# Talking-heads attention and a squared-ReLU network on one core: more work in four 64x64 tiles of TensorE, and a new order of its units

## The chip, the cores and the metric

The kernel runs on one core of one Trainium2 chip, as one launch. The metric is the device time of one execution in microseconds (us); lower is better. The other cores are idle.

## The reference

Batch 8, 12 heads, 448 positions, head size 64; all inputs and the output are float32, and the kernel computes in bf16 with float32 sums.

```python
scores = scale * q @ k.transpose(0, 1, 3, 2)             # (8, 12, 448, 448)
scores = einsum('bhij,hg->bgij', scores, w_pre)          # mixes the 12 heads
attn   = exp(scores - max); attn = attn / (sum(attn) + 1e-9)
attn   = einsum('bhij,hg->bgij', attn, w_post)           # mixes the heads again
x      = (attn @ v) put together to (3584, 768)
h      = maximum(x @ w_in, 0.0)                          # w_in 768 x 2048
out    = (h * h) @ w_out                                 # w_out 2048 x 768
```

## The kernel before

**The stages of one batch.** The 448 query positions are cut into 45 chunks of 10 (CH); a chunk of 10 positions by 12 heads fills the partitions of one softmax block, and two chunks make a pair.

- T (emit_T, matmuls at L771 and L775): TensorE transposes q and k, 28 small transposes to a unit, six units a batch.
- QK (emit_QK, L924): scores of two heads at once for a tile of 128 queries, in two matmuls of 64 rows by 128 columns ("row": two tiles of the array, one above the other); the last 64 queries are done in four tiles of 64x64 ("quad"). ScalarE or VectorE evict them into `stage`.
- Relayout (emit_rel): a DMA issued from SP's queue takes each chunk from `stage` into `dring`, so that heads and positions share the partitions.
- Pre-mixing (emit_pre, L991): four matmuls of 64x64 ("quad") mix the heads of two chunks; ScalarE takes the exponentials with their sums (L1026).
- Post-mixing (emit_post, L1095): 14 short matmuls in two row tiles ("row") mix the heads after the softmax and transpose; the results go to `a2t`. VectorE takes the reciprocals, POOL or VectorE fold them into the weights (L1048, L1059).
- AV (emit_AV, L1157): attention times v. A unit makes two pairs of heads for 22 or 23 chunks (220 or 230 columns) in two tiles side by side of 128 rows by 64 columns ("cols"). The 448 keys are seven blocks of 64, held two and two on the 128 partitions in four slots; the odd block has half of its partitions filled with zeros, in `vraw` and in `vodd`, and is multiplied in two halves of the columns, so that a unit has 20 matmuls. One eviction of two copies follows (xt).
- F1 (emit_F1, L1230; L1209 for batches 0 and 1): x times w_in, ReLU (L1261 or L1262), square (L1271). From batch 2 on a unit has 12 matmuls in two row tiles ("row"); a pair of units sums two blocks of 128 outputs, in two phases in which the row tiles swap their two PSUM banks. For batches 0 and 1 it is "full": the whole array.
- F2 (emit_F2, L1351; L1299 for the last two tiles): h2t times w_out, four units of 16 matmuls ("row") to a tile of 128 tokens, in two phases as in F1; a DMA from POOL's queue writes the tile out.
- In batch 0 the first 22 chunks are made directly (emit_direct, L872, "full").

**What sets the order.** All of it is written out without loops on the chip. A planner (class _Plan) holds every piece as a task with its costs. TensorE's units stand in ten streams (0 transposes, 1 QK, 2 pre-mixing, 3 post-mixing, 4 AV, 5 direct, 6 and 7 F1, 8 and 9 F2), and the string ORDER names, digit by digit, from which stream TensorE takes its next unit. All other tasks are placed by the planner on ScalarE, VectorE, POOL or SP, in the order in which its estimates say that they come ready; tasks marked FLEX go to ScalarE or VectorE, whichever is to end first. The planner also gives each unit its PSUM banks, of eight (_Group, find), and holds estimates for the start and the rate of DMAs (DMA_START, DMA_AHEAD, dma_next), for a change of tiling (MODE_SWITCH) and for TensorE's instruction fetch (FETCH). These estimates are in no instruction: they only decide the order and the engine of the other tasks. Two phases of one sum that swap banks are held apart by a semaphore of TensorE on itself (`t.sync`).

## Time and profile before

| | us |
|---|---|
| median of 3 runs | 525.23 |
| the three runs | 523.72, 525.23, 532.38 |
| the profiled execution | 524.29 |
| its span, first to last instruction | 522.5 |
| TensorE matmul busy | 511.2 |
| ScalarE busy | 441.8 |
| VectorE busy | 423.5 |
| POOL busy | 210.6 |

The profiled execution has 1.79 us outside its span. "PE" is TensorE's matmuls, "PEld" its weight loads, "DVE" VectorE, "ACT" ScalarE, "POOL" GpSimd and "SP" the sync engine. Matmuls overlap in the array, and their ends are modelled, so that a row's duration is longer than what the matmul adds to the time: what a unit costs is read from the start of its first matmul to the start of the next unit. In a timeline row the columns are the start in us, the length in us from the first start to the last end, the engine, the line, the operation with its operands, and how many instructions are merged.

### The profile page before, as it was taken

Reading aid. Unit: us, or ns where it says so; the run is one execution under the profiler, and the core shown is the slowest. Engines: PE = TensorE matmul, PEld = TensorE weight load, DVE = VectorE, ACT = ScalarE, POOL = GpSimd, SP = SyncE. Lnnn points to the kernel's source line nnn. Section 1 sums busy time; section 2 is a strip of 40 time slices with the busy share of each in tenths; the row PEclk is TensorE's granted clock in tenths of the full one; section 3 lists DMA queues with packets and bytes.
Section 4 is the critical chain, followed back from the end, with each engine's and each line's share of the span. In section 5 each row is a group of like instructions: output and inputs, shape, how many; then the busy total and the mean of one; then the engine's idle time right before and its main releaser. Section 6 shows DMA issues by size and latency. Waiting matters only on the chain.

```text
span 522.5 us, 23105 instructions
## 1 busy us (share of the span) xinstructions
PE 511.2 (98%) x9467; PEld 323.7 (62%) x9467; DVE 423.5 (81%) x1181; ACT 441.8 (85%) x1265; POOL 210.6 (40%) x406
## 2 busy tenths in 40 slices
PE   8999999999999999999999999999999999999997
PEld 4455767567767565566456665557556575567874
DVE  7978989799999689978899779977899778967430
ACT  3689999989999898999999889989898898887411
POOL 9614445434642374135532366224643243133000
PEclk9999999999999999999999999999999999999999
DMA  8998999746985589556965599546974567442013
GB/s 157 198 213 160 199 191 195 163 101 134 173 175 115 121 162 178 117 131 140 188 116 109 139 169 182 123 89 148 178 137 102 130 154 132 92 102 63 3 26 101
DMA packets 82391, 71.90 MB, mean 138 GB/s; under 512 B 13371, under 2 KB 79659, under 8 KB 82283
## 3 DMA queue, kind: packets, MB, share of 16 engines
q0 software_dynamic: 36624, 32.81, 38.4%
q1 hardware_dynamic: 45370, 37.38, 29.8%
q8 instruction: 77, 1.26, 1.0%
q10 hardware_dynamic: 288, 0.20, 0.1%
q14 instruction: 32, 0.25, 0.1%
HBM read 45.70 MB, written 11.01 MB: 109 GB/s over the span
## 4 chain that ended last, share of the span: by engine, by line
PE 82%; ACT 10%; DVE 4%; DMA 2%; issue 1%; POOL 1%; SPq 0%; DVEq 0%; ACTq 0%
PE ps L1351 26%; PE ps L1230 20%; PE ps L991 6%; PE ps L1095 6%; PE ps L924 5%; PE ps L1157 5%; PE ps L872 5%; ACT pring L1026 4%; PE ps L1209 3%; ACT a2t L470 3%; PE ps L1299 2%; DMA dring<-stage 2%; PE ps L775 2%; ACT stage L470 1%; DVE stage L471 1%; ACT xt L470 1%
## 5 line engine op out<-in xcount | busy, mean ns | idle before, releaser
L1026 ACT ACTIVATE pring<-ps 128x448 bf16<-128x448 f32 (+1 forms) x368 | 195.4, 560 | 11.7 <-PE ps L872 5.8
L1048 POOL TENSOR_TENSOR wk2s<-wk2b,rinv 128x120 bf16<-128x120 bf16 x179 | 77.1, 433 | 196.4 <-DVE rinv L1041 195.4
L1351 PE MATMUL ps<-w_out_sb,h2t 64*128 64x384 bf16 x1664 | 152.1, 323 | 0.5 <-ACT pring L1026 0.3
L471 DVE CAST a2t<-ps 128x420 bf16<-128x420 f32 x180 | 113.4, 658 | 13.2 <-PE ps L1095 12.2
L1230 PE MATMUL ps<-xt,w_in_sb 64*128 64x448 bf16 (+2 forms) x1344 | 122.5, 323 | 0.2
L470 ACT ACTIVATE a2t<-ps 128x420 bf16<-128x420 f32 x180 | 109.2, 675 | 12.3 <-PE ps L1095 12.1
L471 DVE CAST stage<-ps 128x448 bf16<-128x448 f32 (+1 forms) x173 | 103.5, 616 | 10.2 <-PE ps L924 7.3
L1351 PEld LDWEIGHTS ps<-w_out_sb,h2t 64*128 64x128 bf16 x1664 | 78.8, 94 | 50.6 <-issue 2.8
L470 ACT ACTIVATE stage<-ps 128x448 bf16<-128x448 f32 (+1 forms) x187 | 96.4, 560 | 16.1 <-PE ps L924 15.5
L1230 PEld LDWEIGHTS ps<-xt,w_in_sb 64*128 64x128 bf16 x1344 | 61.2, 94 | 40.3 <-PE ps L924 1.2
L1026 ACT ACTIVATION_READ_ACCUMULATOR pring<-ps 128x1 f32 (+1 forms) x368 | 82.9, 225 | 0.0
L1384 POOL DMA_DIRECT2D out_dram<-osb x52 | 33.6, 652 | 98.3 <-DVE osb L471 32.6
L1095 PEld LDWEIGHTS ps<-wk2s,pring 60*128 60x128 bf16 x2160 | 51.8, 93 | 25.9 <-ACT pring L1026 3.2
L1095 PE MATMUL ps<-wk2s,pring 60*128 60x60 bf16 x2160 | 59.3, 187 | 1.9 <-POOL wk2s L1048 1.6
L1271 DVE TENSOR_TENSOR h2t<-h1t 128x448 bf16<-128x448 bf16 (+2 forms) x176 | 51.8, 323 | 5.2 <-ACT h1t L1261 4.7
L991 PE MATMUL ps<-dring,wk 64*64 64x448 bf16 (+1 forms) x676 | 53.5, 363 | 2.1 <-ACT pring L1026 1.0
L1059 DVE TENSOR_TENSOR ptail<-pring,rinv 128x128 bf16<-128x128 bf16 x169 | 50.7, 300 | 1.9
L1262 DVE TENSOR_SCALAR h1t<-ps 128x448 bf16<-128x448 f32 (+2 forms) x92 | 44.3, 481 | 9.8 <-PE ps L1230 7.1
L1261 ACT ACTIVATE h1t<-ps 128x448 bf16<-128x448 f32 (+2 forms) x84 | 38.3, 460 | 16.2 <-PE ps L1230 12.5
L1041 DVE RECIPROCAL rinv<-sums 128x2 f32<-128x2 f32 x184 | 28.8, 157 | 27.0 <-ACT pring L1026 25.7
L924 PE MATMUL ps<-qkt 64*128 64x448 bf16 (+1 forms) x360 | 50.1, 355 | 0.3 <-DVE qkt L471 0.2
L1209 PE MATMUL ps<-xt,w_in_sb 128*128 128x228 bf16 (+1 forms) x384 | 41.3, 260 | 0.4 <-ACT a2t L470 0.3
(72 smaller groups left out, 557.2 us busy)
## 6 DMA issues: line engine op xcount, KB each, us to landing
dring<-stage SPq DMA_DIRECT2D x309, 105.0 KB
out_dram<-osb POOLq DMA_DIRECT2D x52, 192.0 KB, 3.6
qraw<-in_q_dram POOLq DMA_DIRECT2D x42, 112.0 KB, 5.2
kraw<-in_k_dram POOLq DMA_DIRECT2D x42, 112.0 KB, 5.2
w_in_sb<-in_moe_w_in_dram POOLq DMA_DIRECT2D x8, 384.0 KB, 14.8
vraw<-in_v_dram POOLq DMA_DIRECT2D x24, 128.0 KB
w_out_sb<-in_moe_w_out_dram POOLq DMA_DIRECT2D x8, 384.0 KB, 9.5
vraw<-in_v_dram POOLq DMA_DIRECT2D x24, 96.0 KB
```

The costliest lines, as they stand in the source:

```text
L470: return eng.activation(o, i_, AF.Copy)
L471: return eng.tensor_copy(o, i_)
L924: r_ = eng.matmul(ps[y * w:(y + 1) * w, g.banks[x], 0:S], qkt[r0:r0 + 64, pb, p + y, 0, i0:i0 + w], qkt[r0:r0 + 64, pb, p + y, 1, :], star ...
L991: r_ = eng.matmul(ps[64 * y:64 * y + 64, gr.banks[x], 0:S], wk1[64 * x:64 * x + 64 - R0 * x, :], dring[64 * x:64 * x + 64 - R0 * x, (g0 + ...
L1026: return eng.activation(pring[0:r1, pr, 0:S], ps[0:r1, gr.banks[x], 0:S], AF.Exp, accum_out=sums[0:r1, g, :], **bias)
L1048: return eng.tensor_tensor(wk2s[:, p0:p0 + n, :], i0.to_broadcast([128, n, PR]), rinv[:, p0:p0 + n, :].to_broadcast([128, n, PR]), ALU.mult)
L1059: return eng.tensor_tensor(ptail[:, p0 // 2, :, :], pring[:, p0:p0 + n, 0:PJ], rinv[:, p0:p0 + n, :].to_broadcast([128, n, PJ]), ALU.mult)
L1095: r_ = eng.matmul(ps[:, gr.banks[x], o * PR:(o + 1) * PR], p_, w_, start=True, stop=True)
L1209: r_ = eng.matmul(ps[:, g.banks[0], 0:n], w_in_sb[:, ft, t * 128:(t + 1) * 128], xt[:, ft, c0:c1], start=(ft == 0), stop=(ft == NFT - 1))
L1230: r_ = eng.matmul(ps[:, g.banks[x], 0:n], w_in_sb[64 * y:64 * y + 64, ft, t * 128:(t + 1) * 128], xt[64 * y:64 * y + 64, ft, c0:c1], start ...
L1271: return eng.tensor_tensor(h2t[:, t16, o0:o0 + n], h1t[:, s, 0:n], h1t[:, s, 0:n], ALU.mult)
L1351: r_ = eng.matmul(ps[:, g.banks[hh], 0:FH], h2t[64 * y:64 * y + 64, t16, col:col + 128], w_out_sb[64 * y:64 * y + 64, t16, hh * FH:(hh + 1 ...
```

## The change

1. **Flexible tiling (`other`).** A QK unit of 128 queries, an F1 unit from batch 2 on and an F2 unit (but for the last two tiles) may run in "row" or in "quad". The planner decides when TensorE takes the unit: where the unit before was "quad", this one is "quad" too, with twice as many matmuls of 64 columns; else it stays "row".
2. **AV in quad.** A unit now makes one phase of two pairs of heads: the upper and the lower 64 partitions are separate row tiles that write to two PSUM banks, and a second unit swaps the banks behind a semaphore of TensorE on itself. The half-empty slot is no longer multiplied twice: 16 matmuls to a unit (four groups of four), three groups over all columns and one over half of them, two units where there was one. The unit holds two PSUM banks instead of one, and each pair of heads is evicted by a task of its own.
3. **Planner.** DMA_AHEAD from 3900 to 0, the rate of relayouts beside loads from 47.8 to 45.0, the estimates of the transposes and of w_out's loads; LATE is 0.0 and changes nothing.
4. **Batch 0.** The tiles of queries behind the direct part are 220 to 334 and 334 to 448 instead of 220 to 330 and 330 to 448, so that one chunk is moved by two relayouts.
5. **ORDER.** 998 digits instead of 950 (48 more AV units), all of them new.

```diff
-DMA_AHEAD = 3900.0
+DMA_AHEAD = 0.0
...
-    "0001155500055555555555555555115553115555313555500135555555533155335555511152533552020330"
...
+    "0001555010055555515555155515515553315315555135505551505115555555002353355553355555031213"
...
-                rate = (47.8 / (54.0 + b[2]), 0.72)
+                rate = (45.0 / (54.0 + b[2]), 0.72)
...
     def _commit_pe(self, t, start):
-        if t.mode != self.mode:
-            self.mode = t.mode
+        if t.other is not None and t.other[0] == self.mode:
+            t.mode, held, t.instrs = t.other
+            t.cost = {PE: (held, held + 190.0)}
+        self.mode = t.mode
...
-    NQ0 = 2
-    QT0 = tuple((CH * (ND + x * (NCH - ND) // NQ0),
-                 min(S, CH * (ND + (x + 1) * (NCH - ND) // NQ0))) for x in range(NQ0))
+    NQ0 = -(-(S - CH * ND) // IT)
+    QT0 = tuple((CH * ND + x * (S - CH * ND) // NQ0,
+                 CH * ND + (x + 1) * (S - CH * ND) // NQ0) for x in range(NQ0))
...
                     def fn_qk(eng, en, p=p, g=g, me=me, quad=quad):
                         r_ = None
+                        m = PJ if me[0].mode == "quad" else IT
                         for x, y in QUADS:
-                            if y * w < IT:
+                            if y * m < IT:
                                 r0 = 64 * x
+                                p_, i_ = (p + y, i0) if quad else (p, i0 + y * m)
                                 r_ = eng.matmul(
-                                    ps[y * w:(y + 1) * w, g.banks[x], 0:S],
+                                    ps[y * m:(y + 1) * m, g.banks[x], 0:S],
...
+                    if not quad:
+                        t_qk.other = ("quad", 205.0, t_qk.instrs + 4)
...
-                for p in range(0, NP, 2):
-                    g = _Group(1)
+                for p, ph in ((0, 0), (0, 1), (2, 0), (2, 1), (4, 0), (4, 1)):
+                    g = open_.setdefault(p, _Group(2))
...
+                        for s in range(NM + 1):
+                            for y, kk in QUADS:
+                                x = ph ^ y
+                                h = 2 * (p + x) + kk
+                                rows = slice(64 * y, 64 * y + 64)
+                                o_ = ps[kk * 64:kk * 64 + 64, g.banks[x], 0:w].rearrange(
+                                    "p (y n) -> p y n", y=2)
+                                a_ = a2t[half][rows, :, h, k0 * H5:k1 * H5]
+                                if s < NM:
+                                    a_ = a_[:, s::NM + 1, :]
+                                else:
+                                    a_, o_ = a_[:, NM, :], o_[:, y, :]
+                                v_ = vodd if s == NM and y else vraw[:, :, s, :]
+                                r_ = eng.matmul(o_, v_[rows, h, :], a_,
+                                                start=(ph == 0 and s == 0),
+                                                stop=(ph == 1 and s == NM))
...
-                                2 * NS * (w / 2.4 + 2.9) + 8.0, "cols", g, 4 * (NS + 1))
+                                3.5 * w / 2.4 + 25.0, "quad", g, 4 * (NM + 1))
+                    t_av.sync = before
...
+                        m = 64 if me[0].mode == "quad" else 128
                         for ft in range(NFT):
-                            for y in range(2):
+                            for y, z in QUADS:
+                                if z * m >= 128:
+                                    continue
                                 x = ph ^ y
-                                t = t16 + x
+                                t = (t16 + x) * 128 + z * m
                                 r_ = eng.matmul(
-                                    ps[:, g.banks[x], 0:n],
-                                    w_in_sb[64 * y:64 * y + 64, ft, t * 128:(t + 1) * 128],
+                                    ps[z * m:(z + 1) * m, g.banks[x], 0:n],
+                                    w_in_sb[64 * y:64 * y + 64, ft, t:t + m],
...
+                    t_h.other = ("quad", NFT * (n / 2.4 + 4.3) + 10.0, t_h.instrs + 4 * NFT)
...
+                        t_o.other = ("quad", nk * (FH / 2.4 + 3.7) + 10.0, t_o.instrs + 4 * nk)
```

F2's matmuls (fn_o) are cut in the same way as F1's.

More of the change, by code (lines that the diff above doesn't have):

```diff
@@ L19 @@
 SEM_LAT = 60.0
+LATE = 0.0
 MODE_SWITCH = 102.0
@@ L56 @@
                  "semval", "end", "order", "nwait", "succs", "clock", "avail", "mode", "dma",
-                 "done", "bias", "sync", "group", "instrs", "issued", "later", "two")
+                 "done", "bias", "sync", "group", "instrs", "issued", "later", "two", "other")
     def __init__(self, name, engine, fn, deps, after, cost, prio, sem, seminc, mode, dma,
@@ L81, in __init__ @@
         self.two = False
+        self.other = None
         self.bias = 0.0
@@ L121, in add @@
             mode=None, after=(), dma=None, group=None, instrs=0):
+        if engine not in (PE, SP):
+            cost = {e: (held, lat + LATE) for e, (held, lat) in cost.items()}
         t = _Task(name, engine, fn, deps, after, cost, prio, sem, seminc, mode, dma, group, instrs)
@@ L1470, in program @@
                 if b == 0:
-                    emit_load_w(1, [dir_done[c] for c in range(NDW)])
+                    emit_load_w(1, [dir_done[c] for c in range(min(ND, NDW))])
                     emit_load_v(b)
```

119 lines of the change are left out of this document (62 added, 57 removed).

## Prediction

> **What bounds the kernel now.** I read the page's busy times and chain first, then TensorE's waits, then the stretches, then timelines of TensorE.
>
> ```profile
> span 522.5 us, 23105 instructions
> ...
> PE 511.2 (98%) x9467; PEld 323.7 (62%) x9467; DVE 423.5 (81%) x1181; ACT 441.8 (85%) x1265; POOL 210.6 (40%) x406
> ...
> PE 82%; ACT 10%; DVE 4%; DMA 2%; issue 1%; POOL 1%; SPq 0%; DVEq 0%; ACTq 0%
> ```
>
> TensorE is busy for 98% of the span and 82% of the chain that ended last, so TensorE sets the end. Its named waits are few; the two longest kinds are these (total, times, longest):
>
> ```profile
> PE ps L1095 <- POOL wk2s L1048: 1.6, 2, 1.1
> ...
> PE ps L991 <- ACT pring L1026: 1.0, 1, 1.0
> ```
>
> By stretches (us, then busy of PE, PEld, DVE, ACT, POOL, the granted clock, the share of the DMA engines, GB/s):
>
> ```profile
> 60.00:120.00 60.00, 58.13 (x1113) 40.06 (x1107) 52.56 (x155) 56.38 (x168) 26.54 (x52) 1.00 0.83 164
> ...
> 240.00:300.00 60.00, 58.45 (x1181) 35.13 (x1179) 52.25 (x138) 56.00 (x159) 24.95 (x48) 1.00 0.69 137
> ...
> 480.00:522.00 42.00, 38.85 (x575) 29.77 (x569) 13.63 (x52) 12.07 (x31) 2.47 (x4) 1.00 0.18 47
> ```
>
> ScalarE is at 56 of 60 us in the middle, a close second there; VectorE has 7 to 8 us of 60 free. In the last 42 us TensorE is alone. The clock is full throughout.
>
> **The price of a change of tiling.** Start to start, in TensorE's timeline:
>
> ```profile
> 252.61 0.37 PE L924 MATMUL ps<-qkt 64*128 64x448 bf16 x2
> 252.80 1.32 PE L1230 MATMUL ps<-xt,w_in_sb 64*128 64x448 bf16 x12
> 253.94 0.37 PE L924 MATMUL ps<-qkt 64*128 64x448 bf16 x2
> 254.24 0.38 PE L991 MATMUL ps<-dring,wk 64*64 64x448 bf16 x4
> 254.56 1.31 PE L1230 MATMUL ps<-xt,w_in_sb 64*128 64x448 bf16 x12
> ...
> 258.84 0.57 PE L991 MATMUL ps<-dring,wk 64*64 64x448 bf16 x8
> 259.25 0.39 PE L775 MATMUL ps<-ident,qraw 64*64 64x64 bf16 x28
> 259.46 0.43 PE L775 MATMUL ps<-ident,kraw 64*64 64x64 bf16 x28
> 259.83 1.31 PE L1230 MATMUL ps<-xt,w_in_sb 64*128 64x448 bf16 x12
> ```
>
> A QK unit before another row unit takes 0.19 (252.61 to 252.80); before a quad unit it takes 0.30 (253.94 to 254.24), so the change costs 0.11. Two pre-mixings take 0.41 (258.84 to 259.25): 0.19 streamed, as the row pair of the same 448 columns, and about 0.02 more for the first group behind a change, whose weights were not loaded ahead. The way back, 254.24 to 254.56, is 0.32 less 0.21, again 0.11.
>
> How many changes: I walked ORDER, giving each digit its unit's tiling and, after, the rule of `other`. Before there are 255 changes, 94 of them into quad; after there are 195, 66 of them into quad (the label's 201 would hold the warm-up units, which are in no digit). So 60 fewer at 0.11 make **-6.6**, and 28 fewer first groups at 0.02 make **-0.6**. Bounds: the changes stand on the path only where TensorE would not have waited anyway, so 0 to -7.2.
>
> **AV.** Five units in a row of the batch at 424 us give the price:
>
> ```profile
> 424.17 0.52 PE L1157 MATMUL ps<-a2t,vraw 128*64 128x220 bf16 x8
> ...
> 424.95 0.50 PE L1157 MATMUL ps<-a2t,vraw 128*64 128x220 bf16 x8
> ...
> 426.51 0.52 PE L1157 MATMUL ps<-a2t,vraw 128*64 128x230 bf16 x8
> ...
> 427.31 0.52 PE L1157 MATMUL ps<-a2t,vraw 128*64 128x230 bf16 x8
> ```
>
> A unit takes 0.78 at 220 columns and 0.80 at 230, 0.79 on the mean. It streams eight widths (1800 columns at 225); the two new units stream seven (1575). A column costs 0.19/448 = 0.00042, so 1575 take 0.67; eight groups at 0.003 more give 0.69 to 0.70. 48 units by 0.09 make **-4.3**.
>
> But the second unit of a pair waits for the first's end. What this costs where nothing stands between shows in F1, where two units follow each other twice:
>
> ```profile
> 195.06 2.44 PE L1230 MATMUL ps<-xt,w_in_sb 64*128 64x448 bf16 x24
> 197.34 0.54 PE L924 MATMUL ps<-qkt 64*128 64x448 bf16 x4
> ...
> 208.88 2.62 PE L1230 MATMUL ps<-xt,w_in_sb 64*128 64x448 bf16 x24
> 211.34 0.25 PE L1095 MATMUL ps<-wk2s,pring 60*128 60x60 bf16 x6
> ```
>
> Two units of different sums take 2.28 (195.06 to 197.34); the two phases of one sum, held by the semaphore, 2.46: 0.18 more. In the new ORDER 6 of the 48 AV pairs follow directly; 28 have one unit of 0.19 between, which just covers it; the rest have more. 6 by 0.18 make **+1.1**; if the cover of 0.19 were short by 0.06, 28 more would add 1.7. Nothing but TensorE's own later units is queued behind that wait.
>
> **Quad for QK, F1 and F2.** By the same walk 51 more QK units, 43 F2 units, 34 F1 units of 448 columns and 12 narrow ones turn quad. QK and pre-mixing stream the same 0.19. For F1 and F2 the work is 43*8 + 46*6 = 620 groups of four where pairs stood. Their price in quad is nowhere in the trace; the rows that bear on it are the transposes above, the only long quad run: 28 with a weight load each, seven groups of four. The first unit takes 0.21 (259.25 to 259.46), 0.030 a group; both take 0.47 (to 259.83, less 0.11 for the change), 0.034 a group. 64 columns stream in 0.027, so a group costs 0.003 to 0.007 over its streaming; I take 0.006. The F2 pairs:
>
> ```profile
> 221.41 1.46 PE L1351 MATMUL ps<-w_out_sb,h2t 64*128 64x384 bf16 x16
> 222.71 0.73 PE L924 MATMUL ps<-qkt 64*128 64x448 bf16 x6
> ```
>
> Eight pairs in 1.30, 0.163 each for 384 columns (0.160 streamed): 0.003 over. The difference, 0.003 by 620, is **+1.9**. Ends: 0 if the pairs' price holds, and 620 by the 0.02 of an unprepared first group, +12.4. I take the transposes' value, since they are a run with loads in it.
>
> The page "TensorE: Matmul & The Clock Gate" of the Trainium skill (Part 3, packing small matmuls) says that a weight load runs beside a matmul in flight only in another row group; quad has two tiles in each. By that rule each group would pay its load, and the term would be the +12.4. The transposes at 0.030 to 0.034 do not bear it out; it stays as a rival.
>
> **Instruction fetch.** More matmuls mean more instructions for TensorE: 51*2 + 43*16 + 46*12 + 96*16 - 48*20 = 1918 matmuls, and as many loads, on 9467 of each: a fifth more.
>
> ```profile
> q8 instruction: 77, 1.26, 1.0%
> ```
>
> 77 packets for 18934 instructions are one for about 246; at some 518 us, 92.5 of them leave 5.6 us for each instead of 6.8. That TensorE can run out of code shows here:
>
> ```profile
> 201.47 0.19 PE L1095 MATMUL ps<-wk2s,pring 60*128 60x60 bf16 x1
> 201.83 0.38 PE L1095 MATMUL ps<-wk2s,pring 60*128 60x60 bf16 x11 [0.17 <-issue]
> ```
>
> A post-mixing stops inside its unit, where no semaphore is waited for, for 0.36 where 0.03 is usual. The fetch queue from 89.5 to 105.5 us, and from 195 to 205 us:
>
> ```profile
> q8 instruction: 4, 0.07, 1.7%
> ```
>
> ```profile
> q8 instruction: 2, 0.03, 1.4%
> ```
>
> Four packets in 16 us, one in 4, were in time; in the busier stretch around the stop two in 10 us, one in 5, were not. Walking ORDER with the durations above and cutting every 246 instructions, stretches shorter than 4.0 us add up to a lack of 2.4 us before and 8.4 after; of the 2.4 I find about 1 in the trace, since waits lengthen dense stretches. 1/2.4 of 8.4 is **+3.5**. Ends: 0, and a bound for AV alone: its 96 units of 32 instructions fill 12.5 packets at 0.35 a unit, 2.7 us each where 5 are needed: 2.3 by 12.5 = +29.
>
> The page "Runtime: NRT & Kernel Launch" of the Trainium skill (Instruction fetch mechanics) calls the crossing of such a block mostly hidden. By that the term is 0 and the sum 3.5 lower; the stop at 201.47 is one that was not hidden.
>
> **Waits.** Pre-mixings that follow one another wait for ScalarE's exponentials to free banks:
>
> ```profile
> 75.33 0.38 PE L991 MATMUL ps<-dring,wk 64*64 64x448 bf16 x4
> 76.76 0.38 PE L991 MATMUL ps<-dring,wk 64*64 64x448 bf16 x4 [1.04 <-ACT pring L1026]
> ```
>
> ORDER has 72 direct successions of pre-mixings before and 37 after, since flexible units now stand between. I take a little over half of the 2.6 us of waits quoted at the start: **-1.5**. Ends -4 and +5: AV holds two banks for one, and ScalarE has little room.
>
> **Costed at nothing.** AV's evictions are as many copies as before, of 220 or 230 columns each, shared by two engines and off the path:
>
> ```profile
> L471 DVE CAST xt<-ps x54: 370/395/415, 49.2 to 456.0; 128x220 bf16<-128x220 f32 x30, 128x230 bf16<-128x230 f32 x24
> L470 ACT ACTIVATE xt<-ps x42: 368/408/505, 50.7 to 486.5; 128x230 bf16<-128x230 f32 x24, 128x220 bf16<-128x220 f32 x18
> ```
>
> Were the cover gone, a unit would stand 0.4 us for its bank. One relayout more in batch 0 goes to SP's queue, which holds 309 of the largest kind:
>
> ```profile
> dring<-stage SPq DMA_DIRECT2D x309, 105.0 KB
> ```
>
> It stands beside the direct matmuls of batch 0; uncovered it would cost one pre-mixing's wait, under 1 us. POOL's loads keep their chain. The planner's other estimates move tasks between engines, not their number.
>
> **Sum.** -6.6 -0.6 -4.3 +1.1 +1.9 +3.5 -1.5 = -6.5 against the profiled execution's 524.29 (span 522.5 and 1.79 around it): 517.8. That execution is 0.94 under the median 525.23, so the forecast for a median is 518.7, 1.2% less.
>
> **Rivals.**
> - Fetch is hidden and the waits shrink by 4: 518.7 - 3.5 - 2.5 = 512.7. For it: before, almost all fetches are hidden, and fewer bursts of pre-mixing. Against it: a fifth more code.
> - ScalarE becomes the bound from 60 to 300 us, with 56 of 60 busy: what is saved in those 240 of 522 us (46% of 11.5, about 5) turns into waits: 523.7. Against it: VectorE's free 7 to 8 us, and FLEX.
> - Every quad group pays its weight load: 518.7 + 12.4 - 1.9 = 529.2. Against it: the transposes.
> - Slower: AV in quad outruns the fetch. Two AV units take 0.70 with 64 matmul and load instructions, where one took 0.79 with 40. At the full 29 instead of 3.5 it is 544; from 10 us of stops on it is slower than before, from 20.5 on by over 2%. Against it: 41 AV units stand alone and 20 runs have two, with longer units between.
>
> **How the numbers follow.** Forecast 0.43 (its own range 515 to 523), hidden fetch 0.32, ScalarE 0.12, weight loads 0.07, fetch stops 0.06. Faster by over 2% (under 514.7; 2% is about what a measurement of this kernel can tell from no change) is the second case, 0.32; slower by over 2% (over 535.7) is the last, 0.06; within 2% the other three, 0.62. The range 509 to 530 leaves out the last case and the lower part of the second.
>
> **What would show each step.** The page after should list about 11400 matmuls and 92 packets in the fetch queue. Right: quad F2 units of 32 matmuls at 1.30 to 1.34; AV units at 0.33 to 0.36; a timeline with fewer gaps of 0.11; chain and busy share of TensorE still near 98%. Wrong: F2 quad units at 1.45 (loads exposed), many idle times of TensorE ended by "issue" inside a unit (fetch), or waits of TensorE for ScalarE's evictions in the hundreds of nanoseconds from 60 to 300 us. The sum falls if TensorE's busy time sinks as said but its waits grow by as much.

## The result, and the profile after

The changed kernel takes 533.65 us in the median of four executions, three of them between 532.74 and 533.79; the kernel before takes 526.37 beside it: a ratio of 1.0136, interval 1.009 to 1.0182. One execution took 1263.08 us (as one of dry_nosync's twelve below took 1262.55), at a full clock and for a cause that is not known; the ratios leave these two out, and the median of the other three is 533.51. The change makes the kernel slower by 1.4%, and the time lies above the range that was given. The profiled execution took 532.74 us, 8.45 more than the profiled one of before (524.29), and 14.9 more than the sum of the prediction (517.8).

The page of the changed kernel, the lines that answer to those shown of before:

```profile
span 531.0 us, 26929 instructions
...
PE 508.6 (96%) x11380; PEld 334.0 (63%) x11380; DVE 429.8 (81%) x1184; ACT 443.4 (84%) x1267; POOL 207.9 (39%) x401
...
q8 instruction: 92, 1.51, 1.1%
...
PE 3%; ACT 0%; DVE 0%; issue 0%
```

The counts are as forecast (about 11400 and 92): 11380 matmuls, 92 packets of code. TensorE's busy time fell by 2.6 us although it has 1913 matmuls more, while the span grew by 8.5: TensorE has less to do and stands still longer. The chain breaks off a few per cent from the end in this trace (3% of TensorE and nothing else), so it carries nothing here; what stands still has to be read from TensorE's own rows.

TensorE's waits in the changed kernel (total, times, longest):

```profile
PE ps L1260 <- issue: 4.5, 5, 1.6
PE ps L1109 <- issue: 3.0, 2, 2.3
...
PE ps L1388 <- issue: 1.1, 2, 0.9
PE ps L1174 <- issue: 0.8, 1, 0.8
```

Before, the longest kinds, the warm-up's apart, were waits for POOL and for ScalarE. Now the first places belong to "issue", that is to stops in which no semaphore was waited for, and they fall on every kind of work: here F1, post-mixing, F2 and AV, each once or a few times, and in rows below these QK and transposes. A cause that strikes whatever stands there is hardly in any one of these units.

Stretches of the changed kernel (busy of PE, PEld, DVE, ACT, POOL, the clock, the share of the DMA engines, GB/s):

```profile
60.00:120.00 60.00, 59.08 (x1303) 41.52 (x1305) 54.00 (x161) 57.32 (x177) 25.93 (x52) 1.00 0.84 159
...
240.00:300.00 60.00, 56.50 (x1376) 36.54 (x1369) 52.05 (x135) 52.97 (x153) 24.89 (x50) 1.00 0.69 134
```

From 60 to 120 us TensorE is busier than before (59.1 against 58.1). From 240 to 300 us it loses 2.0 us of busy time against before, and ScalarE, which was to be the rival bound there, falls from 56.0 to 53.0. So ScalarE did not become the bound: it does less in the same time, as it would if TensorE held it up.

Now the place itself, TensorE's timeline of the changed kernel:

```profile
253.52 0.54 PE L1260 MATMUL ps<-xt,w_in_sb 64*128 64x448 bf16 x3
254.51 1.11 PE L1260 MATMUL ps<-xt,w_in_sb 64*128 64x448 bf16 x9 [0.45 <-issue]
...
257.48 1.31 PE L1260 MATMUL ps<-xt,w_in_sb 64*64 64x448 bf16 x24
258.62 0.36 PE L1005 MATMUL ps<-dring,wk 64*64 64x448 bf16 x4
...
260.56 0.19 PE L1109 MATMUL ps<-wk2s,pring 60*128 60x60 bf16 x2
261.43 0.23 PE L1109 MATMUL ps<-wk2s,pring 60*128 60x60 bf16 x4 [0.68 <-issue]
...
262.82 1.32 PE L1260 MATMUL ps<-xt,w_in_sb 64*128 64x448 bf16 x12
264.07 0.38 PE L1005 MATMUL ps<-dring,wk 64*64 64x448 bf16 x4
...
264.91 1.13 PE L1260 MATMUL ps<-xt,w_in_sb 64*64 64x448 bf16 x20
266.82 0.38 PE L1260 MATMUL ps<-xt,w_in_sb 64*64 64x448 bf16 x4 [0.78 <-issue]
...
272.77 0.28 PE L782 MATMUL ps<-ident,qraw 64*64 64x64 bf16 x11 [0.63 <-issue]
```

An F1 unit stops after 3 of its 12 matmuls, a post-mixing after 2 matmuls of a run of 6, an F1 unit after 20 of 24, a transpose after 17 of 28. Counted in the order in which TensorE gets its loads, matmuls and semaphore instructions, all 14 long stops without a semaphore (steps of over 0.3 us from one matmul to the next, the warm-up left out) stand at the same place modulo 256, to one instruction (at the 193rd or 194th of each 256). 256 instructions are what one packet of the fetch queue brings (16.4 KB of 1.51 MB in 92 packets). So these read as stops at the end of the code that is there; the packets, next, bear it out.

The same 6.9 us between two such borders, 254.51 and 261.43, in the DMA view of the changed kernel: first up to 259.1, and then the microsecond from 259.1 on.

```profile
q0 software_dynamic: 716, 0.43, 74.7%
q1 hardware_dynamic: 459, 0.38, 28.4%
```

```profile
q0 software_dynamic: 162, 0.09, 72.4%
...
q8 instruction: 1, 0.02, 5.5%
```

For 4.6 us after the border no code moves: the first view has no row of q8 at all, the DMA engines are full of the POOL queue's loads (q0, 75%) and the relayouts (q1, 28%). The packet comes at 259.13, lasts 0.88, and TensorE goes on 1.42 after its end. Such a fetch takes 6.9 us; at its start TensorE had 6.0 us of work left (254.51 to 260.56).

**The ledger.** For every group of matmuls I took the time from its start to the next one's and laid it down as streamed work (columns by 0.00042, and up to 0.03 a group above it), as a change of tiling (up to 0.125 where the tiling differs), as a stop (at a 256th instruction, no semaphore), as a wait (the next group has a semaphore to wait for), or as other. The span is 5.4 us longer than each sum in these two kernels: what lies ahead of the first matmul and behind the last. In us:

| | streamed | changes (number) | stops (number) | waits | other | sum |
|---|---|---|---|---|---|---|
| before | 474.5 | 27.8 (263) | 0.4 (2) | 12.5 | 1.9 | 517.1 |
| after | 472.8 | 20.8 (201) | 12.7 (14) | 17.8 | 1.4 | 525.5 |
| difference | -1.7 | -7.0 | +12.3 | +5.3 | -0.5 | +8.4 |

The change did what it says, for 8.7 us, and lost 17.6 to code that came late and to waits.

### The profile page after: what moved, and what is told of

The parts are those of the page before. It is cut to its first block, busy times and chain, and to the rows that moved or that the text cites. A ratio compares the mean times of both kernels' runs of the same rounds, so it can differ in the third digit from the quotient of the medians.

```text
span 531.0 us, 26929 instructions
## 1 busy us (share of the span) xinstructions
PE 508.6 (96%) x11380; PEld 334.0 (63%) x11380; DVE 429.8 (81%) x1184; ACT 443.4 (84%) x1267; POOL 207.9 (39%) x401
## 3 DMA queue, kind: packets, MB, share of 16 engines
q8 instruction: 92, 1.51, 1.1%
## 5 line engine op out<-in xcount | busy, mean ns | idle before, releaser
L1040 ACT ACTIVATE pring<-ps 128x448 bf16<-128x448 f32 (+1 forms) x368 | 197.6, 565 | 12.7 <-PE ps L1005 7.9
L1388 PE MATMUL ps<-w_out_sb,h2t 64*64 64x384 bf16 (+1 forms) x2352 | 153.8, 323 | 1.3 <-issue 1.1
L478 DVE CAST a2t<-ps 128x420 bf16<-128x420 f32 x196 | 122.8, 659 | 11.3 <-PE ps L1109 10.3
L1260 PE MATMUL ps<-xt,w_in_sb 64*64 64x448 bf16 (+5 forms) x1896 | 124.9, 324 | 4.6 <-issue 4.5
L1388 PEld LDWEIGHTS ps<-w_out_sb,h2t 64*64 64x64 bf16 (+1 forms) x2352 | 88.1, 101 | 41.6 <-issue 2.3
L477 ACT ACTIVATE a2t<-ps 128x420 bf16<-128x420 f32 x164 | 100.0, 675 | 11.0 <-PE ps L1109 10.1
L1260 PEld LDWEIGHTS ps<-xt,w_in_sb 64*64 64x64 bf16 (+1 forms) x1896 | 67.5, 101 | 38.6 <-issue 6.6
L1005 PE MATMUL ps<-dring,wk 60*64 60x448 bf16 (+1 forms) x676 | 59.8, 360 | 1.2 <-DVE stage L478 0.4
L1293 ACT ACTIVATE h1t<-ps 128x448 bf16<-128x448 f32 (+2 forms) x102 | 45.6, 469 | 18.2 <-PE ps L1260 16.4
L936 PE MATMUL ps<-qkt 64*64 64x448 bf16 (+1 forms) x460 | 54.4, 355 | 1.5 <-issue 0.7
L1174 PE MATMUL ps<-a2t,vraw 64*64 64x230 bf16 (+3 forms) x1344 | 46.8, 253 | 1.6 <-issue 0.8
L1294 DVE TENSOR_SCALAR h1t<-ps 128x448 bf16<-128x448 f32 (+2 forms) x74 | 36.6, 496 | 13.1 <-PE ps L1260 11.4
```

Of the source, the lines that this page charges most:

```text
L477: return eng.activation(o, i_, AF.Copy)
L478: return eng.tensor_copy(o, i_)
L936: r_ = eng.matmul(ps[y * m:(y + 1) * m, g.banks[x], 0:S], qkt[r0:r0 + 64, pb, p_, 0, i_:i_ + m], qkt[r0:r0 + 64, pb, p_, 1, :], start=True ...
L1005: r_ = eng.matmul(ps[64 * y:64 * y + 64, gr.banks[x], 0:S], wk1[64 * x:64 * x + 64 - R0 * x, :], dring[64 * x:64 * x + 64 - R0 * x, (g0 + ...
L1040: return eng.activation(pring[0:r1, pr, 0:S], ps[0:r1, gr.banks[x], 0:S], AF.Exp, accum_out=sums[0:r1, g, :], **bias)
L1174: r_ = eng.matmul(o_, v_[rows, h, :], a_, start=(ph == 0 and s == 0), stop=(ph == 1 and s == NM))
```

## The experiments

Two theories at first. **Code:** the stops are the loss; the new kernel runs the same work through a fifth more instructions, and the fetch does not keep up. **Waits:** TensorE's waits, above all AV's second phase behind its first and AV's two banks, set the pace; a stop only takes up time that would be waited out anyway. The first eight runs take out one part each; the other eight take the two suspected costs away. The kernel before ran beside each of the five groups of runs, on the same chip (medians 525.75, 525.65, 526.37, 526.61 and 525.16); the ratios are to it.

**1. Code alone.** The kernel before, with each F2 matmul cut into two of 192 columns: 1664 matmuls and as many loads more, no change of order, of tiling or of sums.

```diff
-                                for y in range(2):
+                                for z, y in ((0, 0), (0, 1), (1, 0), (1, 1)):
+                                    c = z * FH // 2
-                                        ps[:, g.banks[hh], 0:FH],
+                                        ps[:, g.banks[hh], c:c + FH // 2],
```

> The kernel before, with each matmul of F2 (L1351) cut into two of 192 columns: the same work in the same tiling and order, but 1664 more matmuls and as many weight loads, 3328 instructions more, nearly as many as the change adds (3826). Theory (TensorE runs out of code): the array itself pays about 832 groups at 0.0025 = 2 us; the fetch queue goes from 77 to 90 packets, and stops inside units at every 256th instruction appear, 6 to 12 us in all: 533 to 540. Rival (the new order or the quad tiling makes the loss, not the amount of code): 528 to 529, and no more stops than before.

Measured: 532.21 us, ratio 1.0101 (1.0031 to 1.0171); profiled span 531.7. The ledger against before: streamed +2.0, stops +8.0 (9 of them), waits -0.2. The waits of TensorE in this kernel:

```profile
PE ps L1352 <- issue: 2.8, 3, 1.4
PE ps L1230 <- issue: 2.3, 1, 2.3
PE ps L1095 <- POOL wk2s L1048: 1.6, 2, 1.1
```

The stops are in the range that was forecast (6 to 12), the time is just under its own (533 to 540). Two rows of "issue" have put themselves ahead of the wait for POOL that led before. Instructions alone, with 90 packets for 77, bring the stops. The longest (2.3 idle, at 324.25 us) is not in F2, whose matmuls were cut, but in an F1 unit as it was: it is the border that is paid for, whatever unit stands there.

**2. Less traffic beside the code.** From batch 2 on, the loads of q, k and v bring one row each; in the changed kernel and in the one before. The lines for v are shown; q and k are cut alike. The rest of that data is left out.

```diff
+                    if b >= 2:
+                        i_ = bass.AP(v.tensor, (b * H + h0) * S * D + t0 * D,
+                                     [[NT * D, 1], [S * D, 4], [1, D]])
+                        o = vraw[64 * u:64 * u + 1, h0:h0 + 4, 0, :]
```

> The changed kernel, whose loads of q, k and v from batch 2 on move a single row in place of the whole (the rest of q, k and v of these batches is left out; all instructions stay). Theory (the code's packets stand behind the loads of POOL's queue): the time from a block's border to its packet falls to about 1 us, the 13 us of stops at borders fall below 4, and the time falls to 519 to 524. Rival A (fetch has a time of its own that loads do not touch, the code is simply too much): stops stay at 10 us or more, 528 to 534. Rival B (the stops are only where waits would be anyway): stops vanish, but the time stays over 529.

> The kernel before with the same light loads (q, k and v of batches 2 to 7 left out but for one row). It had under 1 us of stops, so by the fetch theory it gains only what lighter transfers give to relayouts: 522 to 526, and the changed kernel with light loads is to lie 0 to 6 us below it, as the forecast without fetch had it. If it gains as much as the changed kernel does (10 us), the loads cost both kernels by another way than fetch.

Measured: after 530.16, ratio 1.0083 (1.0054 to 1.0113); before 524.82, ratio 0.9991 (0.9967 to 1.0015). The stops of the changed kernel fall from 12.7 to 5.9, its waits go from 17.8 to 18.7. So about half of the stops comes from the loads that move beside the code; the relayouts (q1) are left as they were. The theory's time (519 to 524) did not come, and its stops (below 4) not quite: the time lies where both rivals had it. A part of the 5.3 us between the two light kernels is the granted clock, the share of its full clock that TensorE was allowed: 0.990 to 0.997 in every execution of light_after, 0.999 or more in eight of ten of light_before.

**3. The row tiling alone.** The changed kernel and its order, with `other` left out, so that QK, F1 and F2 always run in rows; AV stays in quad.

```diff
-                        t_qk.other = ("quad", 205.0, t_qk.instrs + 4)
+                        t_qk.other = None if True else ("quad", 205.0, t_qk.instrs + 4)
```

(one of three such lines; the same in F1 and F2)

> The changed kernel with flexible tiling taken out (QK, F1 and F2 always in row tiles), AV in quad and the new ORDER kept: 370 changes of tiling instead of 195, and 2684 instructions fewer. Theory: stops at borders fall from 13 to about 3 us, the 175 changes at 0.11 bring back 19 us, which makes 540 to 545: the flexible tiling does save its changes, and pays for them in code. Rival (quad units are slow in themselves): under 534.

Measured: 541.04, ratio 1.0288 (1.0216 to 1.0359). Against after: changes +19.3 (376 for 201), stops -9.0, waits -1.6, streamed -1.6. The time is as forecast (540 to 545). In this order the flexible tiling saves 19.3 us of changes, and pays 10.6 for it in stops and streamed work.

**4. An order that leaves the code time.** The changed kernel; digits of ORDER were moved about by the planner's own reckoning with a longer fetch (4.7 us), until few borders were short. One of ORDER's twelve lines is shown; all were changed.

```diff
-    "2336372010716233627100726123673137424424002922391391119118333832282182192239139133931414"
+    "2336372100716233617200712623672137434420240922391119319118333832281282192239339131931412"
```

> The changed kernel with an ORDER of its own: digits were moved about while the planner's FETCH held a fetch at 4.7 us and more in place of 4.0, with the rest as it is. It has 222 planned changes of tiling instead of 201 and as much code. Theory (the planner took fetch as too short, and its order put dense code where the code was late): stops at borders fall from 12.7 to under 6 us, 21 changes more cost 2.3, so 527 to 530. Rival (the amount of code makes the stops, in whatever order): stops stay over 9 us, 533 or more.

Measured: 533.19, ratio 1.0167 (1.0118 to 1.0217). The stops are down to 1.7 (forecast: under 6), the waits up from 17.8 to 24.6, changes +2.5; the time is the rival's (533), not the theory's (527 to 530). TensorE's waits in this kernel:

```profile
PE ps L1005 <- ACT a2t L477: 1.1, 3, 0.5
PE ps L936 <- DVE h1t L1294: 0.9, 1, 0.9
...
PE ps L1260 <- issue: 0.8, 1, 0.8
```

Here the theory of the code alone fails: an order that gives the fetch time puts units beside each other that wait for banks and for the engines that empty them. Avoided by order, the stops turned into waits.

**5. The parts alone.** Three kernels, each with an order moved by the same search: the kernel before as it is (a control for the search), the kernel before with AV in quad, and the changed kernel with before's AV and quad only where no row unit comes next. Of each edit only the lines that tell it are shown.

```diff
 order_alone: before, ORDER moved
 avq_alone:   before + quad AV
+                for p, ph in ((0, 0), (0, 1), (2, 0), (2, 1), (4, 0), (4, 1)):
+                    g = open_.setdefault(p, _Group(2))
 flex_alone:  after - quad AV, and
+                elif then == "row":
+                    t.other = None
```

> The kernel before with nothing but its ORDER moved about in the same way, as the control for the other three: 291 planned changes instead of 263. 28 changes cost 3.1 if nothing else moves; theory: waits fall by about as much, 523 to 529.

> AV in quad without flexible tiling: QK, F1 and F2 as before, the ORDER of before with 48 digits for AV's second units, moved about in the same way. 292 planned changes, 1171 instructions more than before. Theory (the two phases of AV wait for each other and for their two banks, and save 3 us of streaming): 29 changes +3.2, streaming -3, waits +2 to +5, stops under 3: 528 to 534. Rival (AV gains the 4.3 us of the forecast, the loss is flexible tiling's): 521 to 526.

> Flexible tiling without the new AV: AV as before (cols, 20 matmuls to a unit), QK, F1 and F2 in quad only where the next unit of fixed tiling is not row; the ORDER of before, moved about in the same way. 276 planned changes (263 before), 412 instructions more than before. Theory: with so little more code the stops stay under 2 us; 13 changes cost 1.4: 524 to 529. Rival (quad is slow in itself or makes waits): over 531.

Measured: the control 528.77, ratio 1.007 (1.0041 to 1.0099); AV in quad 535.19, ratio 1.0181 (1.0145 to 1.0217); flexible tiling 532.55, ratio 1.0149 (1.0089 to 1.0209). The control is where it was forecast (523 to 529), the other two lie above their forecasts (528 to 534, 524 to 529). No order that I found by the planner's reckoning is as good as the one before had, so neither part can be called worth a gain or a loss by the ratio alone. The ledgers say more: the kernels split by their AV. Every kernel with AV in quad had waits of 16 to 25 us up to here (after 17.8, light_after 18.7, rows_only 16.2, order_fetch 24.6, avq_alone 21.4); every one without has 11 to 15 (12.5, 11.9, 12.3, 14.8, 10.9). As the orders differ as well, this is a pattern and not a proof.

**6. The wait between AV's phases.** In both phases each row tile takes the bank of its own number, so the second need not wait for the first; order, placement and instructions stay. The sums then lack the terms of the other row tile.

```diff
-                                x = ph ^ y
+                                x = y
-                    t_av.sync = before
+                    t_av.sync = []
```

> The changed kernel; in both phases of an AV unit each row tile takes the bank of its own number (x = y), so that no two row tiles ever add into one bank, and the second phase no longer waits for the first. The order, the planner's placement and every instruction's size are as in the changed kernel (the sums lack the terms of the other row tile, so half of each product is left out of its place). Theory (the wait for the first phase's end is a cost of its own on TensorE's path): the waits of AV behind AV (1.7 us, 11 of them) and of AV behind a pre-mixing that stands between the phases (0.7 us, 12) vanish, TensorE's waits fall from 17.8 to about 15.4, and the median from 533.6 to about 531.2. Rival (TensorE's waits are set by the engines that free its banks; the phase wait only takes up time that would be waited out a little later): the waits move to the next bank, and the median stays at 533 to 534.

> As the run before it, and in addition the q, k and v loads of batches 2 and above bring one row each instead of all (the rest of that data is left out), as in the earlier run with light loads at 530.2. If the stops for code and the phase waits are separate costs on one path, this kernel stands 2.4 below that: about 527.8, and still above the kernel before with light loads (524.8), by the remaining stops of 5.9 us. If both only hide other waits, it stays at 529.5 to 530.5.

> The changed kernel in the order moved so that TensorE rarely runs out of code (stops 1.7 us, waits 24.6, 533.2), with the same edit of AV: no wait between the phases. There AV behind AV waits 2.8 us (13 times) and AV behind a pre-mixing 0.5. Theory of separate costs: about 530 us. Rival, that the waits are those of the banks whatever the order: 532.5 to 533.5, with TensorE's waits still at 23 or more.

Measured: nosync 537.71, ratio 1.0185 (1.0123 to 1.0247), light 530.23, ratio 1.0079 (1.0051 to 1.0107), in the order of 4 534.11, ratio 1.0146 (1.0094 to 1.0197). By the medians none is faster than its counterpart with the wait (533.65, 530.16, 533.19). AV's own waits did go: AV behind AV from 1.73 to 0.79 us in nosync, from 2.82 to 0.16 in fetch_nosync. But TensorE's waits in all stayed within 0.5 us of what they were in both, so other units waited instead, as the rival had it; and the stops grew: 12.7 to 16.2, 5.9 to 8.5, and 1.7 to 5.3. TensorE's timeline of nosync, at the F1 unit that stopped at 254.51 in the changed kernel:

```profile
256.43 0.54 PE L1260 MATMUL ps<-xt,w_in_sb 64*128 64x448 bf16 x3
258.59 1.11 PE L1260 MATMUL ps<-xt,w_in_sb 64*128 64x448 bf16 x9 [1.62 <-issue]
```

It is the same matmul; the step to it from the matmul before is 1.97 us for 0.80. A likely reading, which no run shows by itself, is that AV that need not wait comes to the end of its code sooner. Taking the phase wait away bought nothing here. How much it cost is open for nosync: its executions were granted a clock of 0.990 to 0.996 (0.97 in three of the 60 us stretches of the profiled one), the changed kernel's 0.994 to 0.999, so a part of its time is that. Executions at 0.999 or more can be compared in the order of 4, where they took 532.71 and 533.79 without the wait, 531.89 and 534.39 with it.

**7. Code in time.** The decisive pair: from batch 2 on the relayouts too bring one row each, so that far less moves when code is fetched: from 120 to 480 us the loads' queue (q0) has 10% of the DMA engines for 33% in the changed kernel, and the relayouts' (q1) 4% for 34%. Order, placement and instructions of each kernel stay.

```diff
+                    if b >= 2:
+                        eng.dma_start(dring[o:o + H, slot, :],
+                                      stage[r0:r0 + 1, n % 2, :, :]).then_inc(sem.handle, 16)
+                        return
```

> The kernel before; from batch 2 on, the q, k and v loads bring one row each and the relayouts (dring from stage) one row's heads instead of all (the rest of that data is left out), so that the DMA engines are nearly free of the kernel's own traffic when TensorE's code is fetched. The order and the placement stay. It had next to no stops at the 256th instructions (0.4 us), so this changes little by either theory: 523.5 to 525.5 (524.8 with light loads alone).

> The same edit in the changed kernel. Theory (the code of TensorE, fetched beside the loads and the relayouts, is what keeps the changed kernel above the one before): the stops, 12.7 us as it is and 5.9 with light loads, fall to 1 or less; TensorE's streamed work and changes of tiling, 493.6 us, and waits of 18 to 19 then give 521 to 523, at or below dry_before. Rival (the stops only take up time that is waited for other engines anyway): the stops go, the waits grow to about 25 as in the moved order, and it stays at 528 to 530, 4 us and more above dry_before.

> As dry_after, and AV without the wait between its phases (x = y; the terms of the other row tile are left out). With the stops gone nothing but the engines' own waits can take up what the phase wait leaves: if that wait is a cost on the path, 2 us below dry_after; if the next wait for a bank takes it up, the same within 0.7.

Measured: dry_before 524.03 (ratio 0.995, 0.9923 to 0.9976), dry_after 525.56 (0.9972, 0.9942 to 1.0001), dry_nosync 526.71 (0.999, 0.996 to 1.0021). The profiled execution of dry_after took 520.88, that of dry_before 524.23. The page of dry_after:

```profile
span 519.1 us, 26929 instructions
...
PE 507.2 (98%) x11380; PEld 336.2 (65%) x11380; DVE 428.4 (83%) x1184; ACT 441.1 (85%) x1267; POOL 196.9 (38%) x401
...
q0 software_dynamic: 19920, 20.47, 21.2%
q1 hardware_dynamic: 17338, 11.57, 9.5%
q8 instruction: 92, 1.51, 1.2%
```

The same 11380 matmuls and 92 packets of code, TensorE back at 98%. Its timeline, the units that stopped at 254.51, 261.43 and 266.82 in the changed kernel:

```profile
249.31 1.30 PE L1272 MATMUL ps<-xt,w_in_sb 64*128 64x448 bf16 x12
250.45 0.35 PE L944 MATMUL ps<-qkt 64*128 64x448 bf16 x2
...
255.56 0.24 PE L1121 MATMUL ps<-wk2s,pring 60*128 60x60 bf16 x6
255.64 1.30 PE L1272 MATMUL ps<-xt,w_in_sb 64*128 64x448 bf16 x12
...
259.38 1.32 PE L1272 MATMUL ps<-xt,w_in_sb 64*64 64x448 bf16 x24
260.52 0.36 PE L944 MATMUL ps<-qkt 64*64 64x448 bf16 x4
```

Each runs through: 1.14 for the F1 units, 0.08 for the half of the post-mixing. In the ledger the stops are 1.1 us for 12.7, and against dry_before it reads streamed -2.0, changes -6.9, stops +1.0, waits +4.5, sum -3.4. TensorE's waits are those of the changed kernel, to 0.2 us: here the stops went and no waits came in their place. What the expectation said of the time came true for the profiled execution (521 to 523 forecast, 520.9), not for the median: the executions of dry_after spread from 520.9 to 531.

**8. The same from batch 1 on.** To see whether that spread is late code in the first 110 us, where the traffic had been left.

```diff
-                    if b >= 2:
+                    if b >= 1:
```

> The kernel before with the loads of q, k and v and the relayouts cut to a row from batch 1 on already, not from batch 2 (the rest of that data is left out). Nearly no stops were there to lose: 522.5 to 524.5 (dry_before 524.0).

> The same in the changed kernel. dry_after's profiled execution took 520.9, but its others 522 to 531, median 525.6. If these spread because code still comes late at times in the first 110 us, where the traffic was left as it is, then with it cut from batch 1 on the executions draw together at 519 to 523, below dry1_before. If the spread and the remainder have another cause, the median stays at 524 to 527, above dry1_before.

Measured: dry1_before 522.27 (ratio 0.9936, 0.9907 to 0.9966), dry1_after 524.28 (0.9983, 0.9963 to 1.0003), the executions now from 521.0 to 525.7. The median is where the second theory had it (524 to 527, above dry1_before). In the ledger: streamed -1.8, changes -6.9, stops +2.7, waits +6.9, sum +0.9. Of the stops, 2.2 us are one, at 57 us, where the loads of batch 0 and of the weights are whole. TensorE's timeline of dry1_after:

```profile
57.02 0.25 PE L1121 MATMUL ps<-wk2s,pring 60*128 60x60 bf16 x5 [2.04 <-issue]
```

The border before it was at 49.74; the packet came 5.0 us later.

What the spread follows is the granted clock, which stands on record beside each execution (in dry_after the two executions at 0.990 are the longest):

| | at 0.999 or more: number, us, median | below: number, us |
|---|---|---|
| dry_before | 10, 522.2 to 525.1, 524.0 | 0 |
| dry_after | 4, 520.9 to 524.7, 522.2 | 8, 525.0 to 531.1 |
| dry_nosync | 2, 521.3 and 521.8 | 9, 524.7 to 529.0 |
| dry1_before | 9, 521.4 to 524.1, 522.3 | 0 |
| dry1_after | 3, 521.0 to 523.1, 522.2 | 9, 523.9 to 525.7 |

So late code in the first 110 us is not shown to make the spread. At the same clock dry_after is 1.9 us below dry_before, and dry1_after is level with dry1_before.

**What follows.** By the medians the changed kernel stands 7.3 us above the one before. With the traffic away and at the same clock it stands 1.9 below (from batch 2 on) or level (from batch 1 on). So late code, shown by taking away what makes it late, accounts for the whole loss; these comparisons rest on three or four executions of the changed kernel, sorted by clock afterwards. In the medians of all executions the changed kernel stays 1.5 and 2.0 us above, and that goes with the lower clock that the changed kernel is granted more often there; why it is granted less is not known. The edit also brings every tile sooner; the kernel before, which had no stops to lose, gained 2.6 and 2.9 us by it (ratios 0.995 and 0.9936), and the comparison of the two dry kernels leaves that out.

The second finding is that waits take most of what the change saves even when the code is in time: of 8.9 and 8.7 us saved in streamed work and changes, 4.5 and 6.9 in the two dry pairs. Which part of the new AV or of the new order sets them is open. The phase wait alone does not: dry_nosync has 1.5 less of waits than dry_after and 2.7 more of stops, and at the same clock 521.3 and 521.8 us for 522.2, within the 0.7 us that its rival allowed.

## Why the prediction was wrong, point by point

The sum gave 517.8 for a profiled execution that took 532.74. The step that failed most is the fetch of instructions, taken at +3.5 and measured at +12.3; the second is the waits, taken at -0.4 with the phases' wait and measured at +5.3. By its own steps:

- **Changes of tiling: right.** -6.6 and -0.6 forecast, -7.0 in the ledger, for 62 fewer. Quad F1 ahead of quad takes 1.14 (257.48 to 258.62), row F1 ahead of quad 1.25 (262.82 to 264.07): 0.11, the price that was used.
- **Quad groups: right.** +1.9 forecast, by 0.003 a group. F2 in the changed kernel:

```profile
236.50 1.46 PE L1388 MATMUL ps<-w_out_sb,h2t 64*128 64x384 bf16 x16
237.90 0.57 PE L1005 MATMUL ps<-dring,wk 64*64 64x448 bf16 x8
...
238.64 1.53 PE L1388 MATMUL ps<-w_out_sb,h2t 64*64 64x384 bf16 x32
239.98 0.39 PE L1005 MATMUL ps<-dring,wk 64*64 64x448 bf16 x2
```

  In quad 1.34 (238.64 to 239.98), in rows 1.40 less 0.10 for the change behind it (236.50 to 237.90). Over all such units the mean is 1.326 and 1.304, 0.0028 a group of four. The rival that each group pays its weight load would have read 1.45. The rule of the Trainium skill that it rested on, "TensorE: Matmul & The Clock Gate" (Part 3, packing small matmuls), is not borne out by these rows for the loads of quad groups.
- **AV: too much forecast.** -4.3 was reckoned from a unit of 0.35; the trace has 0.37 at 230 columns and 0.355 at 220, so 48 pairs save 3.1. With this, streamed work fell by 1.7 instead of 2.4.

AV units of the changed kernel, then two with a pre-mixing between the phases:

```profile
71.33 0.53 PE L1174 MATMUL ps<-a2t,vraw 64*64 64x230 bf16 x13
...
71.70 0.51 PE L1174 MATMUL ps<-a2t,vraw 64*64 64x230 bf16 x13
...
72.30 0.53 PE L1174 MATMUL ps<-a2t,vraw 64*64 64x230 bf16 x13
```

```profile
247.40 0.36 PE L1005 MATMUL ps<-dring,wk 64*64 64x448 bf16 x4
247.64 0.53 PE L1174 MATMUL ps<-a2t,vraw 64*64 64x230 bf16 x13
```

- **The wait between the phases: short.** From 71.33 to 71.70 one unit follows that of another pair, 0.37; from 71.70 to 72.30 the second phase follows its own first, 0.60. The wait costs 0.23 to 0.24 where F1 had shown 0.18. And a unit of 0.19 does not quite cover it: 0.24 from 247.40 to 247.64, so 0.05 more, which is the prediction's "short by 0.06".
- **Waits: the sign was wrong.** -1.5 was taken for pre-mixings that wait less in a row. They did (pre-mixing behind pre-mixing 2.0 to 1.3, post-mixing behind post-mixing 1.5 to 1.1 us in the ledger by pairs). (The list of before that it starts from leaves out one kind between the two it shows, 1.5 us of the warm-up.) Not forecast were the waits around AV: AV behind AV +1.7, QK behind AV +1.1, pre-mixing behind AV +0.8, AV behind pre-mixing +0.2, and QK behind pre-mixing +0.6. A further 0.8 are transposes that wait behind the warm-up; dry_before has them too. Together with the phases' +1.1 the forecast was -0.4, measured +5.3. The bound of +5 that was given to this term, "AV holds two banks for one", is where it ended; that the banks are the cause is argued from which pairs wait, and no run gave AV other banks.
- **Instruction fetch: the step that failed most.** +3.5 was taken, +12.3 came. The working had each border with 4.0 us for its fetch, a lack of 8.4 by the walk through ORDER, and scaled this by 1/2.4, because before only 1 of a reckoned 2.4 was found. Both halves failed. The scale failed: before, 0.4 us of stops are found in the ledger, after, 12.7, more than the walk's unscaled 8.4. That waits in dense stretches had hidden the rest before is argued; the runs without the phase wait fit it: 1.2 us of AV's waits less and 3.5 more of stops in nosync, 2.8 less and 3.6 more in fetch_nosync. And 4.0 us is no constant: from the border until TensorE can go on (the packet's delay, its length, and 1.42 us behind it) the mean from 110 us on is 3.7 us before, 4.4 after, 3.5 in dry_after, and nearly 7 at the worst border shown. The time between borders has a mean of 5.6 us after and 6.6 before, and the densest tenth is under 4.1 and 5.0. Before, then, even the dense tenth was longer than a mean fetch; after, it is not.
- **Where the bound for AV lay.** The slower rival, AV in quad outruns the fetch, names the mechanism that came to pass: it put the point from which the change is slower at 10 us of stops, and 12.3 came. Its place was only partly right: of TensorE's rows of issue above, 0.8 us stand in AV units and most in F1 and post-mixing, and rows_only, whose AV is in quad as well, has 3.7 us of stops. It is the sum of finer work that outruns its code, not AV alone.
- **ScalarE as the bound, hidden fetch: refuted.** ScalarE is less busy than before from 240 to 300 us (53.0 for 56.0). On the page "Runtime: NRT & Kernel Launch" of the Trainium skill (Instruction fetch mechanics), whose rule is that crossing a block is mostly hidden: of 92 borders here 14 were not, for 12.7 us.

The walk's own 8.4 us, unscaled, would have been the better figure for the fetch; with it the sum comes to 522.7, and with the +5 that stood as the end of the waits to 529.2. Each end was named, but the range was drawn as if they could not come together, and here both came. That one cause, more and finer work on TensorE, brings both is argued: the stops were taken away by less traffic, the waits by nothing that was tried.

## What to carry to other kernels

A change that saves time by cutting matmuls finer is paid for in code: count its instructions per stretch, divide by the block of 256, and compare the shortest intervals, not the mean, with the time that the trace of before shows from a border to the end of its packet, and 1.4 us more. Stops of TensorE in the middle of a unit without a semaphore, at the same place modulo 256, are the sign. How a stop is taken away matters: a new order put 6.8 us of waits in the place of 11.0 us of stops, less traffic took 11.6 us of stops and put no waits there. Compare executions at the same granted clock before a difference of 2 us is given a cause. A small saving in an engine that is 98% busy is easily lost to any of these.

## What the runs showed of the hardware that was not expected

- After a stop, TensorE goes on 1.3 to 1.5 us (median 1.42) after the end of the packet with its next 256 instructions; with most of the traffic gone it is 1.4 to 1.5 still, at the two stops of dry_after.
- The packet does not come at once: the delay from the border to it is 0 to 4.7 us in the changed kernel. From 110 us on the longest, 4.6 us at 254.51, stands beside the POOL queue's loads at 75% of the DMA engines; on the mean q0 holds 54% where the delay is over 2.7 us and 12% where it is under 0.8. Traffic is not all of it: at 436.2 us the delay is 3.6 us while q0 moves nothing and q1 holds 7%.
- A wait of TensorE for its own earlier matmuls costs 0.23 to 0.24 us where nothing stands between, and still 0.05 behind a unit of 0.19.
- Groups of four 64x64 matmuls, each with a weight load, run in F2 at 0.163 us from group to group for 0.160 streamed, as the pairs in rows do (0.163); with the step to the next unit, eight groups take 1.326.
- The granted clock is not the same for kernels of nearly the same work: under 0.999 in 8 of 12 executions of dry_after and 9 of 12 of dry1_after, in none of the 19 of dry_before and dry1_before. In dry_after the executions below took 525.0 to 531.1 us for 520.9 to 524.7.
